# Attention with memory and a two-layer network on one core: unscaled exponentials and a division behind the product with V in the first two chunks

## The chip, the cores and the metric

The kernel runs on one core of a Trainium2 chip. The metric is the time of one execution on the device, in microseconds: 1301.19 us, the median of three runs (1300.96 to 1301.51). The profile shown is one further execution of the same kernel, taken with the hardware profiler.

The engines are named as the profile names them: PE is TensorE's matmul and PEld its load of a stationary operand, DVE is VectorE, ACT is ScalarE, POOL is GpSimd. Each of them works through its own list of instructions in order.

## What is computed

For 8 batches and 8 heads, with 576 positions of width 64, causal attention is mixed with a read of a memory matrix; the result, 4608 rows of 512, then goes through two weight matrices (512 x 2048 and 2048 x 512). Cut to what matters:

```
scores = q @ k.T / sqrt(D), causal;  a = exp(scores - max);  a /= a.sum(-1) + 1e-9
local = a @ v
q_p = phi(q)                      # phi(x) = max(x, 0) + min(exp(x), 1)
mem_out = (q_p @ M_prev) / (q_p @ z_prev + 1e-6)
g = 1 / (1 + exp(-beta))          # one number for each head
x = g * mem_out + (1 - g) * local
h = x @ w_in;  out = max(0.01 * h, h) @ w_out
```

q, k, v and the memory come as 32-bit floats, the weights as 64-bit floats.

## The kernel before, in words

A batch is done in two chunks of queries: chunk 0 of a batch has 320 queries against 320 keys (tiles of 64, 128 and 128 queries with 64, 192 and 320 keys), chunk 1 has 256 queries against 576 keys (two tiles of 128 with 448 and 576 keys). There are 16 chunks of 8 heads. The network of a chunk (class `Moe`, 16 steps of `first` and `second`) runs on TensorE while the next chunk's attention is done, and it splits every operand into a high and a low part, since its matmuls take a rounded 32-bit type: the low part is what rounding left over.

While the first two chunks run, the 32 weight tiles are converted from 64-bit floats: on each, `load_weight` spends two operations of ScalarE, three or four of VectorE (lines 290 to 301) and one or two of GpSimd. The attention of these two chunks (`full`, set by `PLAIN = 2`) runs in plain 32-bit floats on TensorE and needs no low parts of its operands.

One head of attention (`attention`): the score matmul (line 472), then `top` on VectorE (line 480) adds the mask and takes the row's extreme, `exp` on ScalarE (line 496) makes the exponentials and their sum, and then for each tile of queries three VectorE operations follow: `inv` (line 501) adds 1e-9 to the sum and multiplies it by 1/(1-g), `inv2` (line 506) takes the reciprocal, and `scale` (line 509) multiplies the whole row of exponentials by it. On GpSimd, `mem` (line 512) multiplies phi(q) by `rn`, the reciprocal of its product with z and of 1/g (lines 428 to 434), into 64 columns in front of the exponentials in the same tile `pp`. `turn` (line 526) transposes `pp` on TensorE in blocks of 128, ScalarE copies the blocks to `pt` (line 541), and `pv_full` (line 565) multiplies `pt` with M_prev and V, which lie one behind the other in `raw`. The result `o` is copied to its high part `xh` on ScalarE (line 568), and VectorE subtracts to get the low part `xl` (line 571), both as the network's input.

The order of the work isn't written by hand. `Plan` lists all steps with what they read and write, a duration each and a priority; a list schedule over the engines then sets the order on each engine, and that order is fixed when the program is built. Attention goes ahead of the weights in the first chunk, and the network's matmuls come last in priority. Tiles with a tag share a ring of buffers, so that a step waits until an earlier user of its buffer is done. TensorE's results lie in banks: `h` (one), `s` (one), `t` (a ring of two) and `acc0` to `acc3`.

## Time and profile before

| | |
|---|---|
| median of three runs | 1301.19 us |
| the profiled execution's span | 1298.5 us |
| PE, busy share of the span | 96% |
| DVE | 73% |
| ACT | 65% |
| POOL | 61% |

The runs' times include what lies around the span: the median is 2.7 us above the span shown, and the sums below are made against the span and then moved by these 2.7 us. The busy time of PE is that in which some matmul was in flight, so that PE can be busy and yet be fed too slowly. The page's 40 slices show the two stages of this kernel: in the first seven VectorE's digits are 7, 9, 9, 9, 8, 7 and 7 with PE between 7 and 8, and from there on PE stands at 9 to the end. When a row of a group gives a mean duration, successive operations of one engine overlap a little, so that the sum of durations is more than the time that they take.

### The profile page before, as it was taken

What the parts mean: (1) busy time and instruction counts of PE and PEld (TensorE: products, weight loads), DVE (VectorE), ACT (ScalarE), POOL (GpSimd) and SP (SyncE); (2) the same over time, 40 slices, a digit from 0 to 9 for tenths busy, and PEclk for the clock granted to TensorE, in tenths of its full rate; (3) what the DMA queues carried; (4) which work ended last, traced back from release to release, by engine and by line L of the source; (5) the groups of instructions that cost most, each with busy time, mean ns of one, the idle gap of its engine ahead of it and who ended that gap; (6) DMA issues with size and microseconds to landing.
All of it is one profiled execution on the core that took longest, in us unless ns stands there. A gap on an engine that the chain in (4) does not pass through costs nothing.

```text
span 1298.5 us, 26483 instructions
## 1 busy us (share of the span) xinstructions
PE 1243.6 (96%) x8896; PEld 1159.7 (89%) x8896; DVE 951.5 (73%) x3131; ACT 837.7 (65%) x2395; POOL 796.8 (61%) x1152
## 2 busy tenths in 40 slices
PE   7778889999999999999999999999999999999998
PEld 4566779999899999999999999999999999999998
DVE  7999877877788866778578785787767776777311
ACT  7656667766777766767576765667666675776322
POOL 4687757666666665756566665666657575666222
PEclk9899999999999999999999999999999999999999
DMA  6444422212222222222122221222221221212000
GB/s 240 156 145 152 152 74 70 98 68 74 91 82 93 66 70 77 80 88 70 38 96 84 79 70 51 87 69 90 70 74 69 87 79 41 98 65 81 1 21 17
DMA packets 32535, 107.61 MB, mean 83 GB/s; under 512 B 3728, under 2 KB 11920, under 8 KB 32400
## 3 DMA queue, kind: packets, MB, share of 16 engines
q1 hardware_dynamic: 32400, 105.92, 24.1%
q8 instruction: 71, 1.16, 0.4%
q14 instruction: 64, 0.52, 0.1%
HBM read 96.47 MB, written 9.44 MB: 82 GB/s over the span
## 4 chain that ended last, share of the span: by engine, by line
PE 69%; DVE 16%; POOL 6%; issue 5%; ACT 3%; DMA 0%; POOLq 0%; SPq 0%; ACTq 0%; DVEq 0%
PE h L620 24%; PE acc L620 24%; PE t L526 7%; PE o L584 6%; PE s L476 5%; DVE pp L509 3%; DVE pp L480 2%; PE s L472 2%; POOL gl L660 2%; DVE g L651 1%; ACT pp L496 1%; POOL qk L381 1%; DVE tawi L298 1%; DVE pt L544 1%; DVE tawo L298 1%
## 5 line engine op out<-in xcount | busy, mean ns | idle before, releaser
L620 PE MATMUL h<-xh,wih 128*128 128x256 f32 (+1 forms) x1024 | 321.4, 314 | 7.8 <-DVE g L651 6.0
L660 POOL TENSOR_TENSOR gl<-g,gh 128x320 fp32r<-128x320 f32 (+1 forms) x256 | 214.0, 836 | 184.3 <-ACT gh L655 158.1
L620 PE MATMUL acc<-gh,woh 128*128 128x256 f32 (+1 forms) x1024 | 321.1, 314 | 0.3
L620 PE MATMUL h<-xl,wih 128*128 128x256 f32 (+1 forms) x1024 | 302.6, 296 | 0.9 <-DVE xl L571 0.9
L620 PE MATMUL acc<-gl,woh 128*128 128x256 f32 (+1 forms) x1024 | 302.3, 295 | 0.9 <-POOL gl L660 0.8
L620 PE MATMUL h<-xh,wil 128*128 128x256 f32 (+1 forms) x1024 | 302.2, 295 | 0.0
L620 PE MATMUL acc<-gh,wol 128*128 128x256 f32 (+1 forms) x1024 | 301.5, 294 | 0.0
L496 ACT ACTIVATE pp<-pp,st 128x448 f32<-128x448 f32 (+3 forms) x320 | 180.4, 564 | 67.6 <-DVE st L480 61.9
L651 DVE TENSOR_TENSOR g<-h,g 128x320 f32<-128x320 f32 (+1 forms) x256 | 115.9, 453 | 135.2 <-ACT g L646 133.6
L646 ACT ACTIVATE g<-h 128x320 f32<-128x320 f32 (+1 forms) x256 | 104.7, 409 | 163.6 <-PE h L620 142.3
L620 PEld LDWEIGHTS h<-xh,wih 128*128 128x128 f32 x1024 | 193.4, 189 | 18.1 <-DVE g L651 10.9
L620 PEld LDWEIGHTS acc<-gh,woh 128*128 128x128 f32 x1024 | 193.0, 188 | 7.2 <-ACT os L693 1.5
L541 ACT CAST pt<-t 128x256 fp32r<-128x256 f32 (+4 forms) x392 | 141.1, 380 | 87.4 <-PE t L526 83.0
L620 PEld LDWEIGHTS acc<-gl,woh 128*128 128x128 f32 x1024 | 193.2, 189 | 3.8 <-POOL gl L660 1.8
L620 PEld LDWEIGHTS h<-xl,wih 128*128 128x128 f32 x1024 | 193.9, 189 | 2.5 <-DVE xl L571 1.5
L526 PE MATMUL t<-ident,pp 128*128 128x128 f32 (+1 forms) x960 | 168.1, 277 | 26.5 <-DVE pp L509 11.6
L620 PEld LDWEIGHTS h<-xh,wil 128*128 128x128 f32 x1024 | 193.2, 189 | 0.0
L620 PEld LDWEIGHTS acc<-gh,wol 128*128 128x128 f32 x1024 | 192.6, 188 | 0.0
L509 DVE TENSOR_SCALAR pp<-pp,st 128x448 f32<-128x448 f32 (+3 forms) x320 | 187.7, 587 | 5.5
L544 DVE TENSOR_TENSOR pt<-t,pt 128x256 fp32r<-128x256 f32 (+4 forms) x392 | 160.0, 426 | 31.2 <-ACT pt L541 28.7
L480 DVE CUSTOM_DVE_ANT_0 pp<-s,mask 128x448 f32<-128x448 f32 (+3 forms) x320 | 136.6, 428 | 47.7 <-PE t L526 23.0
L512 POOL TENSOR_TENSOR pp<-ph,st 128x64 f32<-128x64 f32 (+1 forms) x320 | 102.1, 324 | 107.7 <-DVE st L434 50.3
(63 smaller groups left out, 2252.9 us busy)
## 6 DMA issues: line engine op xcount, KB each, us to landing
raw<-raw SPq DMA_DIRECT2D x64, 672.0 KB, 4.0
raw<-raw SPq DMA_DIRECT2D x64, 544.0 KB, 3.6
wrwi<-w_in_bits SPq DMA_DIRECT2D x16, 512.0 KB, 3.5
wrwo<-w_out_bits SPq DMA_DIRECT2D x16, 512.0 KB, 3.3
out_t<-os SPq DMA_DIRECT2D x32, 160.0 KB, 1.8
out_t<-os SPq DMA_DIRECT2D x32, 128.0 KB, 1.7
braw<-beta_b SPq DMA_DIRECT2D x1, 4.0 KB, 1.6
```

The source lines that it names most:

```text
L480: nc.vector.tensor_tensor_reduce(out=pp()[:rw, D + k0 : D + k0 + kn], in0=s()[:rw, :kn], in1=mask[:rw, mo : mo + kn], scale=-0.0625 if ful ...
L496: nc.scalar.activation(out=pp()[:rw, D : D + n], in_=pp()[:rw, D : D + n], func=AF.Exp, scale=-1.0, bias=stat(kl_), accum_out=stat(2))
L509: nc.vector.tensor_scalar(out=pp()[:rw, D : D + n], in0=pp()[:rw, D : D + n], scalar1=stat(2), scalar2=None, op0=ALU.mult)
L512: nc.gpsimd.tensor_tensor(out=pp()[:rw, :D], in0=ph3()[:rw, ii, :], in1=rn()[:rw, ii : ii + 1].to_broadcast([rw, D]), op=ALU.mult)
L526: nc.tensor.transpose(t()[:, (j - j0) * rw : (j - j0 + 1) * rw], pp()[:rw, j * P : (j + 1) * P], ident[:rw, :rw])
L541: nc.scalar.copy(part(0), tv())
L544: nc.vector.tensor_tensor(out=part(1), in0=tv(), in1=f32r_bits(part(0)), op=ALU.subtract)
L584: nc.tensor.matmul(o()[:, c0[j] : nq], vt()[:, j, :], pt()[:, t, cols(j, c0[j]) : cols(j, nq)], start=n == 0, stop=n == len(mm) - 1)
L620: nc.tensor.matmul(dst(), l(), r(), start=start and k + j == 0, stop=stop and k + j == len(ops) - 1)
L646: op("ACT", act(n, True), q, lambda: nc.scalar.activation(out=g()[:, :n], in_=hp()[:, :n], func=AF.Copy, scale=0.01), r=[hp[0]], w=[g[0]])
L651: lambda: nc.vector.tensor_tensor(out=g()[:, :n], in0=hp()[:, :n], in1=g()[:, :n], op=ALU.max),
L660: lambda: nc.gpsimd.tensor_tensor(out=gl()[:, :n], in0=g()[:, :n], in1=f32r_bits(gh()[:, :n]), op=ALU.subtract),
```

## The change

In the first two chunks (`full`):

- `inv`, `inv2` and `scale` are gone. The exponentials stay unscaled in `pp`. When the last tile of a head has its sums, three small VectorE operations (`sum_1`, `sum_2`, `sum_3`) add 1e-9 to the sums of all tiles, multiply `rn` by them and take their reciprocals.
- `mem` now waits for `sum_2`, because the memory's part must be multiplied by the sum that is divided away later. The transposes of all tiles of a head (`turns`) are listed behind it.
- `v_gate` puts the gate on V: ScalarE multiplies the V part of `raw` by 1-g in place, in two operations, with a table `part` that is made once.
- `spread` transposes each tile's column of reciprocals, repeated over 128 columns, so that a bank `by` holds them along its columns on all rows: three transposes for a head in chunk 0, two in chunk 1. The bank is `h` in chunk 0 and one of the ring `t` in chunk 1.
- The product `o` is copied to a tile `x1` by ScalarE (`x_raw`), multiplied by `by` on VectorE (`x_div`), and then split: the high part on ScalarE as before, the low part on GpSimd (`x_lo`), no longer on VectorE.
- The first tile of chunk 0 is worked on with 128 rows instead of 64.

The diff's core, with comments left out:

```diff
+    part = cst.tile([P, 2, H], F32, name="part")
+    for k in range(2):
+        nc.vector.reciprocal(part[:, k, :], gate[:, 1, :])
+    nc.vector.memset(part[:D, 0, :], 1.0)
...
-        if not full:
+        if full:
+            def v_gate():
+                for j, (c, n) in enumerate(((0, 1), (1, nj - 1))):
+                    v = raw()[:, o_v + c * D : o_v + (c + n) * D]
+                    nc.scalar.activation(out=v, in_=v, func=AF.Copy, scale=part[:, j, h : h + 1])
+            op("ACT", 2 * act(nj * D // 2) + 190, prio, v_gate, r=[raw[0]], w=[raw["v"]])
+        else:
...
+            rows = P if full else rw
...
-            op("POOL", 300, prio, mem, r=[ph[0], st["n"]], w=[pp["f"]])
-            op("DVE", 129, prio, inv, w=[st["l", ii]])
-            op("DVE", 75, prio, inv2, w=[st["l", ii]])
-            op("DVE", dve2(n) + 40, prio, scale, r=[st["l", ii]], w=[pp["s", 0], pp["s", 1]])
+            if not full:
+                op("POOL", 300, prio, mem, r=[ph[0], st["n"]], w=[pp["f"]])
+                op("DVE", 129, prio, inv, w=[st["l", ii]])
+                op("DVE", 75, prio, inv2, w=[st["l", ii]])
+                op("DVE", dve2(n) + 40, prio, scale, r=[st["l", ii]], w=[pp["s", 0], pp["s", 1]])
+            later.append((ii, i, rw, rows, n, pp))
+            if not full:
+                turns(*later.pop())
+        if full:
+            sums = lambda: st()[:, 12 : 12 + ni]
+            def sum_1():
+                nc.vector.tensor_scalar(
+                    out=sums().unsqueeze(2), in0=st()[:, : 4 * ni].rearrange("p (i c) -> p i c", c=4)[:, :, 2:3], scalar1=1e-9, scalar2=None, op0=ALU.add
+                )
+            def sum_2():
+                nc.vector.tensor_tensor(out=rn(), in0=rn(), in1=sums(), op=ALU.mult)
+            def sum_3():
+                nc.vector.reciprocal(sums(), sums())
+            op("DVE", 129, prio, sum_1, r=[st["l", ii] for ii in range(ni)], w=[st["d"]])
+            op("DVE", 129, prio, sum_2, r=[st["d"]], w=[st["n"]])
+            op("DVE", 75, prio, sum_3, r=[st["n"]], w=[st["d"]])
...
+                op("POOL", 300, prio, mem, r=[ph[0], st["n"]], w=[pp["f"]])
+            for x in later:
+                turns(*x)
+        if full:
+            by = bank("t", 2, "by" + u) if hf else bank("h", 1, "by" + u)
...
+            x1 = tile_([P, 320], F32, "os", 1, "x1" + u)
+            def spread():
+                for ii, i in enumerate(tl):
+                    r = sums()[:, ii : ii + 1].to_broadcast([P, P])
+                    nc.tensor.transpose(by()[:, COL[i] : COL[i] + P], r, ident)
+            def x_raw():
+                nc.scalar.copy(x1()[a, :nq], o()[a, :nq])
+            def x_div():
+                nc.vector.tensor_tensor(out=x1()[a, :nq], in0=by()[a, :nq], in1=x1()[a, :nq], op=ALU.mult)
             def x_hi():
-                nc.scalar.copy(xh()[a, p, :], o()[a, :nq])
+                nc.scalar.copy(xh()[a, p, :], x1()[a, :nq])
             def x_lo():
-                nc.vector.tensor_tensor(out=xl()[a, p, :], in0=o()[a, :nq], in1=f32r_bits(xh()[a, p, :]), op=ALU.subtract)
+                nc.gpsimd.tensor_tensor(out=xl()[a, p, :], in0=x1()[a, :nq], in1=f32r_bits(xh()[a, p, :]), op=ALU.subtract)
```

How the instructions stand now, at three places (names: `pp_0_4_1` is chunk 0, head 4, tile 1; `raw`, `st`, `t`, `o`, `by` carry chunk and head likewise; a lone last number counts buffers, and lines are those of each kernel's own file).

VectorE, head 4 of the first chunk, from the first sum of its exponentials on. Before:

```order
L501 TENSOR_SCALAR st_0_4_377<-st_0_4_377,gate 64x1
L428 TENSOR_REDUCE st_0_5_404<-pz_0_5_372 128x3
L506 RECIPROCAL st_0_4_377<-st_0_4_377 64x1
L298 SCALAR_TENSOR_TENSOR tawo_282<-wrwo_214,tawo_282 128x512
L509 TENSOR_SCALAR pp_0_4_0_385<-pp_0_4_0_385,st_0_4_377 64x64
L501 TENSOR_SCALAR st_0_4_377<-st_0_4_377,gate 128x1 x2
L431 TENSOR_SCALAR st_0_5_404<-st_0_5_404,gate 128x3
L506 RECIPROCAL st_0_4_377<-st_0_4_377 128x1
L571 TENSOR_TENSOR xl_0_0_244<-o_0_3_393,xh_0_0_229 64x320
L509 TENSOR_SCALAR pp_0_4_1_390<-pp_0_4_1_390,st_0_4_377 128x192
L506 RECIPROCAL st_0_4_377<-st_0_4_377 128x1
L434 RECIPROCAL st_0_5_404<-st_0_5_404 128x3
```

and now:

```order
L580 TENSOR_SCALAR st_0_4_394<-st_0_4_394 128x3
L432 TENSOR_REDUCE st_0_5_443<-pz_0_5_392 128x3
L633 TENSOR_TENSOR x_0_3_438<-by_0_3_400,x_0_3_438 64x320
L585 TENSOR_TENSOR st_0_4_394<-st_0_4_394 128x3
L435 TENSOR_SCALAR st_0_5_443<-st_0_5_443,gate 128x3
L528 ISA pp_0_5_0_452,st_0_5_443<-s_0_5_0_0_429,mask 128x64
L528 ISA st_0_5_443 128x1
L588 RECIPROCAL st_0_4_394<-st_0_4_394 128x3
L438 RECIPROCAL st_0_5_443<-st_0_5_443 128x3
```

In place of three operations for each tile (501, 506, 509) there are three for the head (580, 585, 588), and the product of an earlier head with its spread reciprocals (633) stands where the subtraction (571) stood. Up to the last such row of the first chunk, eight weight tiles are ahead in VectorE's list now, and six were before.

GpSimd, around the first head of the second chunk. Before:

```order
L309 TENSOR_TENSOR wil_819<-tawi_726,wih_807 128x512
L660 TENSOR_TENSOR gl_0_2_839<-g_0_2_801,gh_0_2_822 128x320
L512 TENSOR_TENSOR pp_1_0_3_731<-ph_1_0_578,st_1_0_713 128x64
L512 TENSOR_TENSOR pp_1_0_4_768<-ph_1_0_578,st_1_0_713 128x64
L425 TENSOR_TENSOR pz_1_1_721<-ph_1_1_591,raw_1_1_145 128x128
L290 TENSOR_SCALAR tawi_864<-tawi_864 128x512
```

and now:

```order
L313 TENSOR_TENSOR wol_857<-tawo_751,woh_842 128x512
L596 TENSOR_TENSOR pp_1_0_3_747<-ph_1_0_645,st_1_0_739 128x64
L596 TENSOR_TENSOR pp_1_0_4_759<-ph_1_0_645,st_1_0_739 128x64
L313 TENSOR_TENSOR wil_891<-tawi_767,wih_868 128x512
L731 TENSOR_TENSOR gl_0_2_920<-g_0_2_862,gh_0_2_884 128x320
L313 TENSOR_TENSOR wol_931<-tawo_787,woh_915 128x512
```

The two products of phi(q) (512, now 596) stood behind nothing but their own phi; now they need the head's sums, and the weights' subtractions (313) and the network's (731) are queued behind them.

TensorE, heads 3 and 4 of the second chunk. Before:

```order
L526 MATMUL t_1_3_4_0_1375<-ident,pp_1_3_4_1296 128x128 x3
L526 MATMUL t_1_3_4_3_1382<-ident,pp_1_3_4_1296 128x128 x2
...
L620 MATMUL acc_0_1_740<-gh_0_8_1325,wol_1257 128x320
L472 MATMUL s_1_4_4_1_1401<-raw_1_4_966 128x256
L565 MATMUL o_1_3_1403<-pt_1_3_1333,raw_1_3_1135 64x256 x4
L565 MATMUL o_1_3_1403<-pt_1_3_1333,raw_1_3_1135 64x128
L526 MATMUL t_1_4_3_0_1423<-ident,pp_1_4_3_1352 128x128 x4
```

and now:

```order
L627 MATMUL by_1_3_1396<-ident,st_1_3_1224 128x128 x2
...
L619 MATMUL o_1_3_1409<-pt_1_3_1370,raw_1_3_1107 64x256 x4
L619 MATMUL o_1_3_1409<-pt_1_3_1370,raw_1_3_1107 64x128
L691 MATMUL h_0_8_1387<-xh_0_0_285,wih_1204 128x320
...
L691 MATMUL acc_0_2_819<-gh_0_7_1354,wol_1155 128x320
L473 MATMUL t_1_4_3_0_1455<-ident,pp_1_4_3_1323 128x128 x4
L473 MATMUL t_1_4_4_0_1464<-ident,pp_1_4_4_1348 128x128 x3
L691 MATMUL acc_0_3_826<-gh_0_7_1354,woh_1117 128x320
```

Before, head 4's first transposes (`t_1_4_3`) need the bank of head 3's middle block; now they need the bank of `by_1_3`, which comes free when head 3 has been divided (`x_div`). In both programs the same matmuls and transposes stand ahead of the second chunk's network (its first matmul, `h_1_0`), with the 40 spreading transposes added.

## Rows read from the trace of the kernel before

**Rows 1.** The table of stretches of the execution, core 0: the stretch from the span's start, its length, then for each engine the busy time and in brackets its instructions, the granted TensorE clock, the DMA share and GB/s.
```profile
0.00:10.00 10.00, 4.48 (x12) 2.87 (x12) 3.29 (x19) 4.76 (x15) 3.41 (x13) 1.00 0.79 296
10.00:50.00 40.00, 33.80 (x144) 18.51 (x143) 38.70 (x161) 29.78 (x105) 23.16 (x35) 0.96 0.51 182
50.00:160.00 110.00, 90.05 (x496) 73.19 (x496) 105.54 (x223) 65.55 (x148) 82.27 (x72) 0.95 0.44 150
160.00:178.00 18.00, 13.86 (x73) 10.36 (x72) 15.42 (x42) 9.20 (x22) 8.88 (x12) 0.91 0.20 72
178.00:300.00 122.00, 120.60 (x908) 115.27 (x908) 96.04 (x335) 86.90 (x258) 83.09 (x128) 1.00 0.25 84
300.00:1200.00 900.00, 887.63 (x6565) 847.89 (x6564) 672.27 (x2306) 610.48 (x1773) 571.12 (x862) 1.00 0.23 76
```

**Rows 2.** The waits in the first 180 us: who waited for whom; in total, how often, the longest.
```profile
POOL wol L309 <- ACT woh L306: 12.8, 6, 4.5
...
ACT wih L306 <- DVE tawi L301: 11.1, 10, 1.9
...
PE t L526 <- DVE pp L509: 8.7, 7, 1.8
```

**Rows 3.** The timeline around 175 us, VectorE's last row on the weights (start, length, what) and then TensorE's first matmul of the second chunk's mixture (its tile is 256 columns wide).
```profile
174.39 0.69 DVE L301 SCALAR_TENSOR_TENSOR tawo<-wrwo,tawo 128x512 int32<-128x512 int32 x1
...
177.76 0.39 PE L620 MATMUL h<-xh,wih 128*128 128x256 f32 x1 [1.11 <-DVE g L651]
```

**Rows 4.** VectorE's groups by line and shape in the first 180 us: those that the change takes away (count | busy us in sum, mean ns of one | idle before). The group with 64 rows holds one instruction of the third chunk beside the eight of the first, and 501 and 506 have 8 more instructions with 64 rows, not shown, of about the same length.
```profile
L509 DVE TENSOR_SCALAR pp<-pp,st 128x576 f32<-128x576 f32 x8 | 8.5, 1059 | 0.0
...
L501 DVE TENSOR_SCALAR st<-st,gate 128x1 f32<-128x1 f32 x32 | 6.5, 207 | 0.2 <-ACT pp L496 0.2
L509 DVE TENSOR_SCALAR pp<-pp,st 128x448 f32<-128x448 f32 x8 | 6.5, 812 | 0.0
...
L506 DVE RECIPROCAL st<-st 128x1 f32<-128x1 f32 x32 | 4.9, 153 | 0.1
...
L509 DVE TENSOR_SCALAR pp<-pp,st 64x64 f32<-64x64 f32 x9 | 4.0, 450 | 0.0
L571 DVE TENSOR_TENSOR xl<-o,xh 64x320 fp32r<-64x320 f32 x8 | 3.9, 487 | 0.6 <-ACT xh L568 0.4
L509 DVE TENSOR_SCALAR pp<-pp,st 128x192 f32<-128x192 f32 x8 | 3.8, 481 | 0.1
...
L509 DVE TENSOR_SCALAR pp<-pp,st 128x320 f32<-128x320 f32 x8 | 3.6, 447 | 0.0
...
L571 DVE TENSOR_TENSOR xl<-o,xh 64x256 fp32r<-64x256 f32 x8 | 3.3, 418 | 0.1
```

**Rows 5.** The timeline (start, length, what) of VectorE in four places and, as the row that begins at 143.26, of GpSimd: multiplications of line 509 at every width while nothing holds them, and one that begins while GpSimd is in a long operation.
```profile
44.57 0.24 DVE L509 TENSOR_SCALAR pp<-pp,st 64x64 f32<-64x64 f32 x1
44.73 0.15 DVE L506 RECIPROCAL st<-st 128x1 f32<-128x1 f32 x1
44.80 0.20 DVE L501 TENSOR_SCALAR st<-st,gate 128x1 f32<-128x1 f32 x1
44.92 0.68 DVE L298 SCALAR_TENSOR_TENSOR tawo<-wrwo,tawo 128x512 int32<-128x512 int32 x1
45.52 0.31 DVE L509 TENSOR_SCALAR pp<-pp,st 128x192 f32<-128x192 f32 x1
...
46.42 0.38 DVE L509 TENSOR_SCALAR pp<-pp,st 128x320 f32<-128x320 f32 x1
...
88.72 0.51 DVE L509 TENSOR_SCALAR pp<-pp,st 128x576 f32<-128x576 f32 x1
...
96.03 0.44 DVE L509 TENSOR_SCALAR pp<-pp,st 128x448 f32<-128x448 f32 x1
...
143.26 1.48 POOL L309 TENSOR_TENSOR wol<-tawo,woh 128x512 fp32r<-128x512 f32 x1 [0.58 <-ACT woh L306]
...
143.51 1.55 DVE L509 TENSOR_SCALAR pp<-pp,st 128x576 f32<-128x576 f32 x1
```

**Rows 6.** VectorE's groups again, same stretch and columns: the small operation on two and on three columns that stands nearest to the ones added.
```profile
L431 DVE TENSOR_SCALAR st<-st,gate 128x2 f32<-128x2 f32 x8 | 5.2, 649 | 0.1
...
L431 DVE TENSOR_SCALAR st<-st,gate 128x3 f32<-128x3 f32 x10 | 2.2, 222 | 0.0
```

**Rows 7.** GpSimd's groups, same stretch and columns: the subtraction whose shape is nearest to the one that moves there.
```profile
L660 POOL TENSOR_TENSOR gl<-g,gh 128x320 fp32r<-128x320 f32 x16 | 16.3, 1017 | 10.5 <-ACT gh L655 10.5
```

**Rows 8.** ScalarE's groups, same stretch and columns: copies of 64, 256 and 320 columns, and a weight tile's two operations.
```profile
L287 ACT ACTIVATE tawi<-wrwi 128x512 f32<-128x512 f32 x16 | 10.8, 673 | 0.0
...
L306 ACT CAST wih<-tawi 128x512 fp32r<-128x512 f32 x16 | 9.9, 618 | 11.3 <-DVE tawi L301 11.1
L541 ACT COPY pt<-t 128x256 f32<-128x256 f32 x24 | 8.6, 368 | 0.6 <-PE t L526 0.6
...
L568 ACT CAST xh<-o 64x320 fp32r<-64x320 f32 x8 | 3.4, 419 | 2.0 <-PE o L565 1.8
...
L541 ACT COPY pt<-t 128x64 f32<-128x64 f32 x8 | 1.7, 210 | 1.0 <-PE t L526 0.9
```

**Rows 9.** TensorE's timeline near the end of the second chunk: five transposes in a row, the product with V behind them (five matmuls, counted as ten records).
```profile
167.91 0.74 PE L526 MATMUL t<-ident,pp 128*128 128x128 f32 x5 [1.73 <-DVE pp L509]
169.08 3.65 PE L565 MATMUL o<-pt,raw 128*64 128x256 f32 x10 [0.44 <-ACT pt L541]
```

More of the change, by code (lines that the diff above doesn't have):

```diff
@@ L521, in attention, with turns, turn @@
+        later = []
+        def turns(ii, i, rw, rows, n, pp):
             for j0, js in BLOCKS[i]:
                 t = bank("t", 2, f"t{u}_{i}_{j0}")
-                def turn(t=t, js=js, j0=j0, rw=rw, pp=pp):
+                def turn(t=t, js=js, j0=j0, rw=rows, pp=pp):
                     for j in js:
@@ new lines, in attention, with mem @@
+        if full:
+            sums = lambda: st()[:, 12 : 12 + ni]
+            def sum_1():
+                nc.vector.tensor_scalar(
+                    out=sums().unsqueeze(2), in0=st()[:, : 4 * ni].rearrange("p (i c) -> p i c", c=4)[:, :, 2:3], scalar1=1e-9, scalar2=None, op0=ALU.add
+                )
+            def sum_2():
[5 more added lines that the diff above has]
+            op("DVE", 75, prio, sum_3, r=[st["n"]], w=[st["d"]])
+            for ii, i, rw, rows, n, pp in later:
+                def mem(ii=ii, pp=pp):
+                    nc.gpsimd.tensor_tensor(
+                        out=pp()[:, :D], in0=ph3()[:, ii, :], in1=rn()[:, ii : ii + 1].to_broadcast([P, D]), op=ALU.mult
+                    )
+                op("POOL", 300, prio, mem, r=[ph[0], st["n"]], w=[pp["f"]])
+            for x in later:
+                turns(*x)
```

111 lines of the change are left out of this document (56 added, 55 removed).

## Prediction

> **What bounds the kernel now.** I read the table of stretches first [rows 1]. Up to 178 us TensorE is not full: it idles 5.5 us of the first 10, 6.2 of the next 40, 20.0 of the 110 after that and 4.1 of the 18 up to 178, 35.8 us together. From there on it is busy for 120.6 us of 122 and 887.6 of 900. So the kernel is a start of 178 us that something else sets, and a rest of 1120.7 us (1298.5 less 177.8) that TensorE sets. In the same table VectorE is busy for 38.7 us of 40 and 105.5 of 110 while ScalarE has 29.8 and 65.6 and GpSimd 23.2 and 82.3: between 10 and 160 us VectorE is the full one. The waits agree [rows 2]: GpSimd waits for ScalarE's rounding of a weight, that rounding waits for VectorE's conversion of it, and TensorE's transposes wait for the scaling that VectorE does. VectorE's last conversion is at 174.39, and the second chunk's network begins at 177.76 [rows 3]. The listing of the order has the same matmuls ahead of that point in both programs, but for 40 spreading transposes. Whatever the change is worth must therefore show as an earlier or later start of that matmul, with the rest of 1120.7 us behind it unchanged.
>
> **What VectorE loses.** Successive rows overlap: a reciprocal of 0.15 begins at 44.73 and the next instruction at 44.80 [rows 5], so I take 0.08 off every instruction. The 40 scalings (line 509) are 8.5 + 6.5 + 3.8 + 3.6 us and 8 of 0.45, 26.0 in sum [rows 4], less 3.2 is 22.8. The 40 of line 501 at 0.207 are 8.3, less 3.2 is 5.1. The 40 reciprocals of line 506 at 0.153 are 6.1, less 3.2 is 2.9. The 16 subtractions (line 571) are 7.2, less 1.3 is 5.9. Together 36.7 us.
>
> **What VectorE gets.** `x_div` has the shape of line 571, with one operand in a bank and one tile, so I put it at the same 5.9 us. `sum_1` and `sum_2` are not in the trace. In chunk 0 they work on three columns, where line 431 takes 0.222 [rows 6]; with a reciprocal of 0.153 [rows 4] and three overlaps off that is 0.36 for a head, 2.9 us for eight. In chunk 1 they work on two, where line 431 takes 0.649 and single-column line 501 takes 0.207: 0.33 to 1.21 for a head, 2.6 to 9.7 us. I take the middle, 6.2, since `sum_2` is of another kind than either row. Added 15.0 us (11.4 to 18.5), net **21.7 us less** on VectorE (18.2 to 25.3). The table `part` is made near 3 us, before the first operands land, and costs nothing; if it were late, it would be three instructions of the size of line 501, 0.6 us.
>
> **What of it comes back.** First, the scalings wait as well as work. Free, they take 0.51, 0.44, 0.38, 0.31 and 0.24 at the five widths, 15.0 us for eight heads of each; the rows sum to 26.0, so 11.0 us are waiting. One that begins at 143.51 takes 1.55 while GpSimd is in an operation from 143.26 to 144.74 [rows 5]. Where the scaling is gone, VectorE's next instruction may meet the same GpSimd operation, so between 0 and 11.0 us come back; I take half, 5.5. Second, the 16 subtractions that move to GpSimd cost there 1.02 us at 320 columns [rows 7] and in proportion 0.81 at 256, 14.6 us. GpSimd has room for that (16.8 us idle in 40, 27.7 in 110 [rows 1]), but each can hold VectorE up: from 0 to half its length, 7.3 us. I take 2.5, nearer to none, because GpSimd has finished much of each before VectorE comes to an instruction that waits.
>
> What the Trainium skill says here ("SBUF — State Buffer", section "SBUF: two separate sides") is that VectorE and GpSimd share a pair of ports as an exclusive lock, held for a whole instruction, and that VectorE needs it in its two-port modes and also with two operands in SBUF. The row at 143.51 agrees. The rule also puts `sum_2` (two operands in SBUF) on the lock and keeps `x_div` (one in a bank) off it; by it alone the sums would stand at their upper end and the time 3.5 us higher.
>
> Third, the first chunk. Its share of the net is 11.0 us (24 scalings with 9.1 after overlaps, 24 of lines 501 and 506 with 4.8, less 2.9). ScalarE gets two operations on V and the copy `x_raw` for each head: 0.21 + 0.37 + 0.42 by copies of 64, 256 and 320 columns [rows 8], 1.0 us, 8 us in chunk 0 and as much in chunk 1. The listing also has two more weight tiles ahead of the last head of chunk 0, 0.67 + 0.62 each on ScalarE, 2.6 us. Against 10.2 us of idle ScalarE between 10 and 50 us that is 10.6: ScalarE is then full, and the chunk can't end much sooner than now. What VectorE saves there is used by the two tiles only, some 4 us (three operations of 0.60 for a tile, after overlap, and a fourth for every second one); between 0 and 7 us of the 11 are lost. I take 3. In chunk 1 ScalarE has 44 us idle of 110, and its 8 us lie beside VectorE.
>
> **What costs nothing.** The 40 spreading transposes at 0.15 (five in 0.74 [rows 9]) are 6 us on TensorE and lie in its 35.8 us of idle time; without that cover they'd cost 6. The first tile's 128 rows change no column count. `mem` now waits for `sum_2`; behind it GpSimd has weights and the network's subtractions queued, whose readers are TensorE's matmuls with the same cover. The bank `h` is taken by `by` through chunk 0, so nine early matmuls of the network move behind it, 9 x 0.15 = 1.3 us of the same idle time. `x1` is one buffer: `x_raw` waits for the `x_lo` of the head before, and the eight heads of chunk 1 are spread over some 120 us.
>
> **Sum.** 21.7 less 5.5, 2.5 and 3 is 10.7 us off the start. The profiled execution's span becomes 1287.8, and the median, 2.7 above the span, becomes **1290.5 us**. With every cost at its lower end it is 1301.2 - 25.3 = 1276, with every one at its upper end 1301.2 - 18.2 + 11.0 + 7.3 + 7 = 1308.
>
> **Rivals.**
>
> *The whole saving arrives.* VectorE has been the full engine for 150 us, and the others have idle time; if neither GpSimd's operations nor ScalarE take anything back, the time is 1301.2 - 21.7 = 1279.5. Against it: ScalarE's sum for chunk 0. Chance 0.18.
>
> *GpSimd's waits take it all back.* All 11.0 us of waiting move to other instructions, the moved subtractions add their 7.3 and the sums stand at 1.21 a head (3.5 more): 21.7 - 21.8 leaves nothing, 1301 us. For it: line 431 takes three times as long on two columns as on three [rows 6]. Against it: line 571 reads a bank and stands at 0.487 and 0.418 on the average [rows 4], no longer than its width asks. This is where the rule of the Trainium skill above would lead. Chance 0.10.
>
> *The transposes stand still, and it is slower.* In chunk 1 `by` and `o` take the ring `t` between one head's transposes and the next's, so TensorE stops in front of a head until the division of the last one is done: product with V (3.65 us in one case [rows 9]), copy, `x_div` behind whatever VectorE has queued. TensorE's busy time up to 178 us is 142.2 [rows 1]; with 6 us of transposes and the 5.5 us until the first operands, 24 us are left, so it decides from 3 us of standing for each of 8 heads. At 4 us each the start grows by 8, to 1309. For it: transposes already wait 8.7 us for the scaling in seven places [rows 2]. Against it: the network's matmuls stand between the heads in most places. Chance 0.06.
>
> **How the numbers follow.** The forecast has 0.66; its own range is 1283 to 1298. The range of 8 in 10 takes in the first rival's time and leaves out the other two: 1279 to 1299. A difference under 0.2% (2.6 us) can't be told from none in this kernel. Faster: the forecast but for 0.02 of its upper tail, the first rival and 0.01 of the second, 0.83. Same: 0.02 and 0.08, 0.10. Slower: 0.06 and the last 0.01, 0.07.
>
> **What would show it.** Right: the first 256-column matmul of the network starts near 167 us instead of 177.8, VectorE's busy time up to there falls by 12 to 20 us, the stretch behind it keeps its 1121 us, and the first chunk's attention ends about where it did. Wrong in a step: conversions of weights (lines 293 to 301 before) that take longer on average by over 0.1 us each would show the waits come back; ScalarE with idle time in the first 50 us would refute the third loss; gaps of several us in TensorE in front of the transposes of chunk 1, ended by `x_div`, would be the last rival. The forecast is wrong as a whole if the first network matmul of the second chunk moves by less than 3 or more than 21 us, or if the rest isn't 1121 us.

## The result, and the profile after

The changed kernel takes 1309.88 us (median of five runs, 1306.68 to 1312.3) against 1301.19: a ratio of 1.0056 [1.0044, 1.0068], 7.3 us slower by that ratio (the two medians are 8.7 us apart). The profiled execution has 1310.51 us and a span of 1308.7. Its table of stretches, with the columns of [rows 1]:

```profile
0.00:10.00 10.00, 4.52 (x12) 3.14 (x12) 2.95 (x17) 5.92 (x20) 2.62 (x10) 1.00 0.79 289
10.00:50.00 40.00, 29.99 (x144) 18.21 (x143) 34.15 (x120) 35.13 (x123) 27.93 (x43) 0.96 0.55 191
50.00:160.00 110.00, 94.11 (x494) 73.56 (x495) 94.94 (x193) 69.23 (x165) 85.56 (x79) 0.91 0.44 144
160.00:178.00 18.00, 15.50 (x90) 12.56 (x90) 16.68 (x42) 11.09 (x29) 13.38 (x14) 1.00 0.31 91
178.00:300.00 122.00, 119.81 (x894) 113.38 (x895) 97.89 (x339) 88.25 (x258) 82.36 (x128) 1.00 0.25 84
300.00:1200.00 900.00, 884.40 (x6528) 843.44 (x6527) 672.63 (x2283) 605.12 (x1758) 561.57 (x853) 1.00 0.23 75
```

VectorE is busy for 148.7 us of the first 178, where it was 163.0 [rows 1]: 14.2 less. Its idle time there rose by the same 14.2, from 15.1 to 29.3. Counted to the start of the second chunk's network in each kernel it is 150.2 us against 162.7, 12.5 less. The work went, and waits came. VectorE's last conversion and the second chunk's network (start, length, what), which answer to [rows 3], stand no earlier:

```profile
174.74 1.08 DVE L305 SCALAR_TENSOR_TENSOR tawo<-wrwo,tawo 128x512 int32<-128x512 int32 x1
...
181.73 0.39 PE L691 MATMUL h<-xh,wih 128*128 128x256 f32 x1
```

The network starts 4.0 us later, and from there to the end it takes 1308.7 - 181.7 = 1127.0 us, 6.3 more than the 1120.7 of before. So in these two profiles, whose spans are 10.2 us apart, two things went wrong, one on each side of that matmul.

The waits of the first 180 us (in total, how often, the longest) answer to [rows 2]:

```profile
ACT woh L310 <- DVE tawo L305: 14.4, 9, 3.3
...
DVE tawi L297 <- POOL tawi L294: 8.8, 3, 4.6
...
POOL wol L313 <- ACT woh L310: 7.8, 6, 2.3
...
PEld t L473 <- POOL pp L596: 6.4, 10, 1.7
```

VectorE now waits 8.8 us for GpSimd's `least` (1.1 us before), and TensorE's loads for the transposes (PEld) wait 6.4 us for GpSimd's `mem`. What VectorE got (count | busy us, mean ns | idle before), as [rows 4, 6] have it for what it had, and GpSimd's moved subtractions, as [rows 7]:

```profile
L585 DVE TENSOR_TENSOR st<-st 128x2 f32<-128x2 f32 x8 | 5.1, 635 | 0.1
...
L633 DVE TENSOR_TENSOR x<-by,x 64x320 f32<-64x320 f32 x8 | 3.9, 487 | 0.6 <-ACT x L630 0.2
...
L633 DVE TENSOR_TENSOR x<-by,x 64x256 f32<-64x256 f32 x8 | 3.3, 417 | 1.3 <-ACT x L630 1.2
L580 DVE TENSOR_SCALAR st<-st 128x3 f32<-128x3 f32 x8 | 3.1, 392 | 3.1 <-ACT pp L544 3.1
L580 DVE TENSOR_SCALAR st<-st 128x2 f32<-128x2 f32 x8 | 2.8, 350 | 0.0
...
L585 DVE TENSOR_TENSOR st<-st 128x3 f32<-128x3 f32 x8 | 1.2, 154 | 0.1
```
```profile
L639 POOL TENSOR_TENSOR xl<-x,xh 64x320 fp32r<-64x320 f32 x8 | 7.3, 912 | 3.5 <-ACT xh L636 3.3
...
L639 POOL TENSOR_TENSOR xl<-x,xh 64x256 fp32r<-64x256 f32 x8 | 6.7, 834 | 1.9 <-ACT xh L636 1.7
```

A useful mark inside the start is the network's first step: VectorE's first `g<-h,g`. It stands at 55.48 us before and at 66.10 after; the sixteenth at 177.22 and 181.19. Cut there, the two tables read (before, then after; columns as above):

```profile
0.00:55.48 55.48, 39.68 (x158) 22.07 (x158) 47.37 (x186) 37.19 (x125) 30.41 (x51) 0.94 0.60 213
55.48:177.22 121.74, 102.27 (x561) 82.62 (x561) 114.81 (x253) 71.33 (x164) 87.23 (x80) 0.96 0.39 133
```
```profile
0.00:66.10 66.10, 44.66 (x187) 28.20 (x188) 50.65 (x156) 50.02 (x164) 44.65 (x64) 0.87 0.55 195
66.10:181.19 115.09, 102.66 (x571) 82.20 (x571) 99.04 (x217) 74.38 (x177) 86.92 (x84) 0.97 0.41 132
```

The first step comes 10.6 us later; the stretch behind it is 6.7 us shorter. In that stretch VectorE does 15.8 us less, but TensorE's 102 us stay, and it has 12 us of idle time left in place of 19.

Where the 10.6 us arise can be read from TensorE's products with V of the last two heads of the first chunk, before:

```profile
45.43 1.59 PE L565 MATMUL o<-pt,raw 128*64 128x320 f32 x6
...
48.69 1.40 PE L565 MATMUL o<-pt,raw 128*64 128x320 f32 x6
```

and after, with what stands between the two:

```profile
46.03 1.40 PE L619 MATMUL o<-pt,raw 128*64 128x320 f32 x6
...
48.05 0.43 DVE L580 TENSOR_SCALAR st<-st 128x3 f32<-128x3 f32 x1
...
48.95 3.32 POOL L596 TENSOR_TENSOR pp<-ph,st 128x64 f32<-128x64 f32 x3 [0.50 <-DVE st L585]
...
52.33 0.90 PE L473 MATMUL t<-ident,pp 128*128 128x128 f32 x3 [1.22 <-POOL pp L596]
...
53.48 2.61 PE L619 MATMUL o<-pt,raw 128*64 128x320 f32 x6 [0.25 <-ACT pt L488]
```

The seventh product ends at 47.43 us against 47.02, so seven heads of the new kind lose 0.4 us together. The eighth ends 6.0 us later than before: its `mem` waits for the sums, then takes 3.32 us for three operations (0.92 for the head before it), and its transposes wait for `mem`. From the end of that product to the first step it takes 10.0 us instead of 5.4. How this last part goes shows in the timeline after (VectorE, GpSimd and ScalarE as named):

```profile
54.51 3.38 DVE L425 SCALAR_TENSOR_TENSOR ph<-ph,pz 128x128 f32<-128x128 f32 x1
...
55.27 1.25 POOL L313 TENSOR_TENSOR wil<-tawi,wih 128x512 fp32r<-128x512 f32 x1
...
56.17 0.42 ACT L630 COPY x<-o 64x320 f32<-64x320 f32 x1 [0.91 <-PE o L619]
56.49 1.25 POOL L313 TENSOR_TENSOR wol<-tawo,woh 128x512 fp32r<-128x512 f32 x1
...
59.38 0.49 DVE L633 TENSOR_TENSOR x<-by,x 64x320 f32<-64x320 f32 x1
...
59.94 0.64 PE L691 MATMUL h<-xh,wih 128*128 128x320 f32 x1 [3.85 <-DVE x L633]
60.37 0.47 PE L691 MATMUL h<-xl,wih 128*128 128x320 f32 x1
...
61.45 0.88 POOL L639 TENSOR_TENSOR xl<-x,xh 64x320 fp32r<-64x320 f32 x1
```

The copy `x_raw` is done at 56.59, but the division stands behind `phi_add` of the next chunk, which GpSimd's operations hold for 3.38 us, and behind two conversions. TensorE stands 3.85 us, then runs the first step's matmuls 0.27 us apart at a granted clock of 0.50 (54 to 60 us), the lower of its two levels.

### The profile page after: what moved, and what is told of

Its sections match the earlier page's. It is cut to its first block, busy times and chain, and to the rows that moved or that the text cites. A ratio compares the mean times of both kernels' runs of the same rounds, so it can differ in the third digit from the quotient of the medians.

```text
span 1308.7 us, 26566 instructions
## 1 busy us (share of the span) xinstructions
PE 1251.7 (96%) x8936; PEld 1166.1 (89%) x8936; DVE 946.7 (72%) x3062; ACT 852.9 (65%) x2443; POOL 806.9 (62%) x1168
## 4 chain that ended last, share of the span: by engine, by line
PE 53%; DVE 6%; POOL 5%; issue 4%; ACT 2%; DMA 1%; POOLq 0%; ACTq 0%
PE acc L691 19%; PE h L691 19%; PE t L473 5%; PE o L655 5%; PE s L524 4%; DVE pp L557 2%; POOL gl L731 2%; POOL qk L385 1%; DMA out_t<-os 1%; DVE pp L528 1%; DVE g L722 1%; POOL qk L388 1%; PE s L520 1%; ACT pp L544 1%; DVE pt L491 1%
## 5 line engine op out<-in xcount | busy, mean ns | idle before, releaser
L544 ACT ACTIVATE pp<-pp,st 128x448 f32<-128x448 f32 (+4 forms) x320 | 180.5, 565 | 74.3 <-DVE st L528 66.5
L528 DVE CUSTOM_DVE_ANT_0 pp<-s,mask 128x448 f32<-128x448 f32 (+4 forms) x320 | 136.8, 429 | 47.0 <-PE t L473 23.6
L557 DVE TENSOR_SCALAR pp<-pp,st 64x64 f32<-64x64 f32 (+4 forms) x280 | 161.5, 577 | 5.3
L473 PEld LDWEIGHTS t<-ident,pp 128*128 128x128 f32 (+1 forms) x960 | 114.3, 141 | 43.2 <-issue 7.8
```

The costliest lines, as they stand in the source:

```text
L473: nc.tensor.transpose(t()[:, (j - j0) * rw : (j - j0 + 1) * rw], pp()[:rw, j * P : (j + 1) * P], ident[:rw, :rw])
L528: nc.vector.tensor_tensor_reduce(out=pp()[:rw, D + k0 : D + k0 + kn], in0=s()[:rw, :kn], in1=mask[:rw, mo : mo + kn], scale=-0.0625 if ful ...
L544: nc.scalar.activation(out=pp()[:rw, D : D + n], in_=pp()[:rw, D : D + n], func=AF.Exp, scale=-1.0, bias=stat(kl_), accum_out=stat(2))
L557: nc.vector.tensor_scalar(out=pp()[:rw, D : D + n], in0=pp()[:rw, D : D + n], scalar1=stat(2), scalar2=None, op0=ALU.mult)
```

## The experiments

The ratio is to the kernel before on the same chip, and 0.001 is 1.3 us. The last three columns are us, each of one profile.

| kernel | ratio [95%] | first step | second chunk's network | from there to the end |
|---|---|---|---|---|
| before | | 55.5 | 177.8 | 1120.7 |
| after | 1.0056 [1.0044, 1.0068] | 66.1 | 181.7 | 1127.0 |
| e1 second chunk only | 1.0027 [1.0018, 1.0036] | 56.8 | 180.1 | 1125.2 |
| e2 first chunk only | 1.0050 [1.0035, 1.0065] | 65.1 | 180.7 | 1126.6 |
| e3 no gate | 1.0069 [1.0055, 1.0083] | 65.7 | 183.6 | 1125.7 |
| e4 mem without sums | 1.0070 [1.0056, 1.0085] | 65.3 | 183.2 | 1127.0 |
| e5 before again | 1.0004 [0.9994, 1.0014] | 55.6 | 178.0 | 1122.0 |
| e6 before, no scaling, second | 0.9965 [0.9952, 0.9978] | 58.1 | 174.2 | 1122.6 |
| e7 before, no scaling, first | 0.9967 [0.9954, 0.9980] | 51.1 | 173.3 | 1122.3 |
| e8 sums spread in ring t | 1.0100 [1.0083, 1.0117] | 70.0 | 185.5 | 1129.3 |
| e9 after, old later order | 1.0045 [1.0031, 1.0060] | 65.7 | 182.8 | 1123.0 |
| e10 division ahead | 1.0071 [1.0058, 1.0084] | 65.3 | 183.6 | 1127.6 |
| e11 tile by tile | 1.0028 [1.0019, 1.0037] | 57.0 | 179.0 | 1126.0 |
| e12 x_lo on VectorE | 1.0032 [1.0021, 1.0044] | 63.1 | 177.0 | 1126.2 |
| e13 e1 with x_lo on VectorE | 1.0006 [0.9998, 1.0015] | 60.0 | 180.5 | 1122.9 |
| e14 before, no scaling at all | 0.9931 [0.9917, 0.9945] | 51.3 | 168.4 | 1122.3 |
| e15 scaling of second on ScalarE | 0.9956 [0.9944, 0.9969] | 54.5 | 171.1 | 1122.0 |
| e16 and the wide ones of first | 0.9976 [0.9967, 0.9985] | 56.5 | 175.3 | 1121.7 |
| e17 before, new later order | 1.0048 [1.0034, 1.0061] | 57.6 | 182.1 | 1126.5 |
| e18 e12 with old later order | 1.0015 [1.0006, 1.0024] | 63.2 | 177.4 | 1123.4 |

**One half of the change at a time.** In e1 and e2 everything that the change adds or takes is made to hang on `new`:

```diff
         full = plain(b, hf)
+        new = full and hf in (1,)     # e2: (0,)
...
-        if full:
+        if new:
             def v_gate():
```

> The change is made in the second chunk alone; the first chunk scales its exponentials as before. Theory A (the first chunk's attention, whose head is now a longer chain through ScalarE, VectorE and GpSimd, ends 10 us later and the start never gets that back): the second chunk's network starts 2 to 8 us before that of the kernel before (170 to 176 us against 177.8), and the time is 1294 to 1300. Theory B (GpSimd, which takes mem behind the sums and the moved subtractions in the second chunk, is the bound there): the network starts at 178 to 184 and the time is 1302 to 1310. Theory C (the later chunks' order, which the planner works out anew, is 6 us worse whatever happens in the start): the time from the network's start to the end is 1126 to 1128 here too, against 1120.7.

> The change is made in the first chunk alone. Theory A: the first chunk's network starts some 10 us later, as in the changed kernel (first step at 66 us against 55.5), the second chunk's network 4 to 10 us later than before, and the time is 1305 to 1312. Theory B: the loss of the first chunk is filled with weights, the second chunk's network starts within 2 us of 177.8, and the time is 1300 to 1303. Theory C: from the network's start to the end 1126 to 1128.

Both halves are slower by themselves. The 10 us of the first step come with the first chunk's half alone, as theory A has it, but only 2.9 us of them reach the second chunk's network (theory A had 4 to 10), and theory A's gain of e1 isn't there: e1 is where theory B put it. Both also take 1125 to 1127 us behind the network's start. Theory C, a new order there, can be the reason in e2 alone, since e1 has the order of before in that stretch.

**The suspected engine loads.** e3 leaves the products of V with the gate out, e4 the products `sum_2`; the order of all other instructions stays.

```diff
-                    nc.scalar.activation(out=v, in_=v, func=AF.Copy, scale=part[:, j, h : h + 1])
+                    pass                                                              # e3
...
-                nc.vector.tensor_tensor(out=rn(), in0=rn(), in1=sums(), op=ALU.mult)
+                pass                                                                  # e4
```

> The changed kernel in its own order, but V is not multiplied by the gate: 32 ScalarE instructions, 10.3 us, are gone. Theory A by way of a full ScalarE (35.1 us of 40 busy between 10 and 50 us): the first chunk ends 3 to 5 us earlier, the second chunk's network starts 3 to 5 us earlier than in the changed kernel, time 1304 to 1307. If ScalarE isn't what holds the first chunk: under 1.5 us, 1308 to 1311.

> The changed kernel in its own order, but the 16 products of the sums with the denominators of phi are left out, so that GpSimd's mem no longer waits for VectorE's sums, and VectorE has 16 instructions less (7 us). If VectorE's work still set the start, the second chunk's network would start 5 to 7 us earlier than in the changed kernel and the time would be 1303 to 1305. If the waits of GpSimd's queue for the sums are what makes VectorE idle (theory B), more than that, 8 to 12 us, time 1298 to 1302. If both lie beside something else (theory A through the chain of copy, division, rounding), 0 to 3 us, 1307 to 1310.

Neither gives anything back, though e3 frees ScalarE of 32 instructions and e4 VectorE of 16. So neither of these two pieces of work is what the start of the changed kernel waits for.

**What the removed work is worth.** e5 is the kernel before, unchanged. e6, e7 and e14 are the kernel before with scalings left out and nothing in their place.

```diff
             def scale(rw=rw, n=n, pp=pp, stat=stat):
+                if (b, hf) == (0, 1):          # e7: (0, 0); e14: if plain(b, hf)
+                    return
```

> The kernel before, unchanged, once more in a profile, because the stretch from the second chunk's network to the end took 1125 to 1127 us in all four variants and 1120.7 before, though the variant of the second chunk alone has the same instructions in the same order there on every engine. Theory D (that stretch scatters from execution to execution, and the 1120.7 was at its lower end): 1122 to 1126 here. Theory E (the changed kernels are slower there, by the place of their tiles in memory or by what the start leaves behind): 1120 to 1121.5. The network's start at 177.8 within 1 us by both.

> The kernel before in its own order, with the 16 scalings of the second chunk left out (some 12 us of VectorE) and nothing put in their place. Theory F (VectorE's work sets the start, as the prediction had it): the second chunk's network starts 8 to 12 us earlier, 166 to 170, time 1290 to 1294. Theory G (from the first network step, near 55 us, TensorE's own work and its waits in order set the pace, 102 us busy of 122, and VectorE only looks full): 0 to 4 us earlier, 174 to 178, time 1298 to 1302.

> The kernel before in its own order, with the 24 scalings of the first chunk left out (some 9 us of VectorE) and nothing put in their place. Theory F: the network's first step 7 to 9 us earlier than 55.5 us and the second chunk's network 7 to 9 us earlier too, time 1293 to 1295. Theory G with a first chunk that is a chain from head to head: the first step 2 to 6 us earlier, and the second chunk's network 2 to 6 us, time 1296 to 1300.

> The kernel before in its own order with all 40 scalings left out and nothing put in their place. If the start is a row of two stretches that each have their own chain, the two gains add: the first network step near 51, the second chunk's network at 169 to 171, time 1292 to 1294.5. If VectorE's work counted in full once both are gone (theory F): 155 to 160, time 1280 to 1284. If something else steps in: 172 to 174, time 1296 to 1298.

e5 takes 1122.0 us behind the network's start, 1.3 more than the same kernel's first profile, at the lower edge of theory D: two profiles of one kernel differ by that much. The halves are worth 4.6 us (e6) and 4.3 (e7), both together 9.0: they add, and theory F falls. (e6's 1296.6 us, by its ratio, lies below theory G's range too.) Cut at the first step as above, e14 reads:

```profile
0.00:51.26 51.26, 37.05 (x158) 21.34 (x158) 39.32 (x161) 36.76 (x125) 31.68 (x51) 0.98 0.66 230
51.26:167.86 116.60, 101.75 (x561) 84.47 (x561) 106.39 (x236) 70.07 (x163) 85.27 (x80) 0.95 0.42 139
```

The scalings had 26.0 us of busy time, 22.8 without overlaps [rows 4]; VectorE's busy time falls by 16.5 and the start by 9.4. The first stretch gives 4.2 us and the second 5.1, where TensorE's 102 us stay.

**The chain of a head in the first chunk.** e8 moves the spread sums to the ring `t`, e10 moves the last division ahead of the three instructions in front of it, and e11 leaves `sum_2` out and lists `mem` and the transposes of a tile beside its exponentials.

```diff
-            by = bank("t", 2, "by" + u) if hf else bank("h", 1, "by" + u)
+            by = bank("t", 2, "by" + u)                                               # e8
...
+        x = [o for o in done if o.fn.__name__ == "x_div"][7]
+        ahead = [o for o in done[: done.index(x)] if o.eng == "DVE"][-3:]
+        done = again(lambda o: x.start + 1 if o in ahead else o.start)                # e10
...
+            if full:
+                op("POOL", 300, prio, mem_, r=[ph[0], st["n"]], w=[pp["f"]])          # e11
...
-            if not full:
-                turns(*later.pop())
+            turns(*later.pop())
```

(`again` lists the steps anew by the key it is given, each behind those it needs.)

> The changed kernel with the spread sums of the first chunk in the ring t and not in bank h, so that the network's first matmuls can go ahead of the last heads again. If bank h is what delays the first network step (66.1 us against 55.5): the step at 60 to 63 us, the second chunk's network 2 to 4 us earlier than 181.7, time 1305 to 1308. If it is the head's longer chain and the ring gets fuller: the step at 66 to 69 us, time 1309 to 1313.

> The changed kernel with one instruction moved: the last division of the first chunk goes ahead of the three VectorE instructions that stood before it (phi_add of the second chunk, held 3.4 us, and two conversions of a weight). If that block is a loss that the start never gets back: the network's first step 2.5 to 3.5 us earlier than 66.1 us, the second chunk's network 2 to 3.5 us earlier than 181.7, time 1306 to 1308. If TensorE's stretch behind it only gets its idle time back: first step 2.5 to 3.5 us earlier, the second chunk's network under 1 us, time 1309 to 1310.5.

> The changed kernel without the product of the sums with the denominators of phi, so that mem and the transposes of a tile need its own exponentials only and are listed tile by tile, as before the change, and not behind the sums of the whole head. If it is the head that waits as a whole (theory A, the longer chain in the first chunk): the first network step falls from 66.1 to 57 to 61 us, the second chunk's network from 181.7 to 174 to 178, time 1301 to 1305. If the chain behind the product with V (copy, division, rounding, GpSimd's subtraction) is what costs: 63 to 66 us, 180 to 183, time 1308 to 1311.

e8 is worse than either reading had it (70.0 us and, by the ratio, 1314.2), so bank `h` alone isn't what delays the first step. In e10 the division and TensorE's first matmul come 3.3 us earlier, and the first step only 0.8; the timeline of e10 shows why:

```profile
56.12 0.49 DVE L651 TENSOR_TENSOR x<-by,x 64x320 f32<-64x320 f32 x1 [2.04 <-ACT x L648]
...
56.67 0.64 PE L709 MATMUL h<-xh,wih 128*128 128x320 f32 x1 [1.09 <-DVE x L651]
...
58.56 0.62 ACT L328 CAST woh<-tawo 128x512 fp32r<-128x512 f32 x1 [2.47 <-DVE tawo L323]
...
59.20 0.46 ACT L654 CAST xh<-x 64x320 fp32r<-64x320 f32 x1
...
60.60 0.86 POOL L657 TENSOR_TENSOR xl<-x,xh 64x320 fp32r<-64x320 f32 x1
```

The rounding `x_hi` now stands in ScalarE's queue behind a weight that waits 2.47 us for the conversions that were moved back. So moving one step of the chain ahead left the next one waiting in another engine's queue. e11 takes some 9 us off the first step, where e4, with the same omission and the order kept, got 0.8: in the first chunk it is the listing by whole heads that costs, as far as one new listing of everything can show it. Its last product with V ends at 45.4 us, 10.7 earlier than after, and the chain from there to the first step still takes 11.6. Of the 9 us only 2.7 reach the second chunk's network, at 179.0 later than the 174 to 178 expected. The time falls by 3.6 us against after and by 2.2 against e9, which has the same later order; the last two intervals overlap.

**The subtractions on GpSimd.** e12 puts `x_lo` back on VectorE, e13 does so in e1, e18 does so in e9.

```diff
-                nc.gpsimd.tensor_tensor(out=xl()[a, p, :], in0=x1()[a, :nq], in1=f32r_bits(xh()[a, p, :]), op=ALU.subtract)
+                nc.vector.tensor_tensor(out=xl()[a, p, :], in0=x1()[a, :nq], in1=f32r_bits(xh()[a, p, :]), op=ALU.subtract)
```

> The changed kernel with the 16 subtractions x_lo on VectorE, as they were, and not on GpSimd. If GpSimd's queue and the operands that both engines want are what holds the start up: the first network step 1 to 3 us earlier than 66.1, the second chunk's network 2 to 5 us earlier than 181.7, time 1304 to 1308, though VectorE does 7 us more. If VectorE's work counts (the prediction's premise): the network 3 to 6 us later, time 1312 to 1316. If neither, within 1.5 us of 1309.9.

> The change in the second chunk alone, with the 8 subtractions x_lo on VectorE and not on GpSimd. If the moved subtractions are what takes the saving back there: the second chunk's network starts 3 to 6 us earlier than the 180.1 of the second chunk alone, 174 to 177, the stretch behind it takes 1122 to 1123.5 (it has the old order), time 1297.5 to 1301.5. If it is the longer chain of the head (sums, mem, copy, division): within 2 us of 180.1, time 1304 to 1307.

Three pairs agree: 0.0024 (after and e12), 0.0021 (e1 and e13), 0.0030 (e9 and e18), 2.7 to 3.9 us (each ratio is good to some 0.0012), though VectorE does more. The planner lists the first two chunks anew each time, so this is the price of the move with the order that goes with it. VectorE's group of line 297 in the first 180 us, after and then in e12, shows the wait that goes:

```profile
L297 DVE TENSOR_SCALAR tawi<-tawi 128x512 int32<-128x512 int32 x16 | 9.5, 611 | 8.9 <-POOL tawi L294 8.8
```
```profile
L297 DVE TENSOR_SCALAR tawi<-tawi 128x512 int32<-128x512 int32 x16 | 10.4, 654 | 0.7 <-POOL tawi L294 0.6
```

e12 is where its first reading put it; e13's time lies between its two readings and can't be told from before. In its one profile e13 started its network no earlier than e1 (180.5), but that execution is 2.6 us above e13's median, and the last section has a part of what delayed it.

**The order of the later chunks.** e9 is the changed kernel with every instruction of the later chunks in the order of before; e17 is the reverse. The old (new) starts in the plan are written into the kernel.

```diff
+        was = {(tuple(x[:4]), x[4]): x[5] for x in json.loads(...)}
+        first = [o for o in done if o.key in was and o.key[0][3] == 2][0]
+        by = first.start - was[first.key]
+        done = again(lambda o: was[o.key] + by if o.key in was else o.start)
```

> The changed kernel with its own order in the first two chunks, but every instruction of the later chunks (third chunk's attention and second chunk's network onwards) is put in the order that it has in the kernel before, on every engine. Theory H (the later chunks' order, which the planner made anew, costs the stretch behind the start some 4 us): from the network's start to the end 1121 to 1123.5, as in the four kernels that have that order by themselves (1120.7, 1122.0, 1122.3, 1122.6), and the time 1304 to 1306.5. Theory I (something else than the order, such as the place of the tiles in memory; the variant of the second chunk alone has that order too and took 1125.2): 1125 to 1127, time 1308 to 1311. The network's start at 181 to 183.5 by both.

> The kernel before, its work and its first two chunks untouched, but every instruction of the later chunks in the order that the changed kernel has there. Theory H (the order costs it): the network of the second chunk at 177 to 179, from there to the end 1125.5 to 1127.5, time 1304.5 to 1307. Theory I (the order doesn't matter, the work of the start or the place of the tiles does): 1120.5 to 1123, time 1300.5 to 1303.

> The changed kernel with its subtractions x_lo on VectorE and the later chunks in the old order. If the two effects add: network at 176 to 178.5, from there 1121 to 1123.5, time 1300 to 1303.5, no different from before. If theory I holds: 1125 to 1127 behind the start, time 1304 to 1307.

The stretch behind the network's start in e9 and in e17:

```profile
182.82:1305.80 1122.98, 1102.56 (x8179) 1055.61 (x8177) 789.87 (x2693) 728.83 (x2107) 678.60 (x1022) 1.00 0.22 71
```
```profile
182.12:1308.60 1126.48, 1104.66 (x8177) 1057.22 (x8177) 795.10 (x2690) 728.11 (x2103) 675.87 (x1020) 1.00 0.21 71
```

With the same matmuls the old order takes 1123 and the new one 1126.5, which is theory H's side. Not all of e17's length is the order's: its first 6 us of that stretch ran at the lower clock, those of before at the higher (e17, then before):

```profile
182.12:188.00 5.88, 5.88 (x25) 5.82 (x25) 1.95 (x9) 2.52 (x8) 3.57 (x6) 0.52 0.32 98
```
```profile
177.76:183.60 5.84, 5.74 (x42) 5.37 (x42) 2.45 (x11) 3.69 (x13) 5.44 (x8) 1.00 0.31 91
```

TensorE has 25 matmuls there in place of 42, and at the 60th matmul e17 is 1.9 us behind. In time the order is worth 1.4 us (after and e9, whose intervals overlap), 2.2 (e12 and e18) and 6.2 (e17 against before; there the network also starts 4.3 us later than before, outside the 177 to 179 expected, so that this isn't the price of the stretch alone). e9's 1307.0 us, by its ratio, misses theory H's time, and e18 ends 2 us above before, not level with it. Ten profiles in the old order took 1120.7 to 1123.4, but e1 and e11, which have it too, 1125.2 and 1126.0. What those two lost is spread over many places; its cause is open.

**Another way to the same saving.** e15 keeps the kernel before, but ScalarE does the second chunk's scalings; in e16 also the eight of 320 keys.

```diff
             def scale(rw=rw, n=n, i=i, pp=pp, stat=stat):
+                if plain(b, hf) and hf == 1:          # e16: and (hf == 1 or i == 2)
+                    p = pp()[:rw, D : D + n]
+                    nc.scalar.activation(out=p, in_=p, func=AF.Copy, scale=stat(2))
+                    return
```

> The kernel before with the 16 scalings of the second chunk on ScalarE (some 10 us of its 44 idle ones between 50 and 160 us) and not on VectorE. If VectorE's work in the second chunk is worth what leaving it out showed: the network 2 to 4 us earlier than 177.8, time 1297.5 to 1300. If ScalarE's place in the chain of a head costs as much: within 1.5 us of 177.8, time 1300.5 to 1303.

> As e15, and the 8 widest scalings of the first chunk (320 keys) on ScalarE too, some 3.5 us of the 10 that it idles between 10 and 50 us. If the first chunk's chain is shortened by that: the first network step 1 to 3 us earlier than 55.5, the network of the second chunk 4 to 6 us earlier than 177.8, time 1295 to 1298. If ScalarE is then what the heads wait for: the first step at 55.5 or later, time as e15 or longer.

e15 beats both kernels: 1296.7 us, 5.7 us (0.9956) under before. Its stretch from 50 to 160 us has ScalarE 10 us busier than [rows 1] and VectorE 4 us less:

```profile
50.00:160.00 110.00, 91.88 (x516) 74.72 (x516) 101.35 (x224) 75.53 (x171) 83.10 (x78) 0.97 0.46 152
```

That is as much as e6 got by leaving the same scalings out (4.6 us). The planner lists the first two chunks anew in e15, and the granted clock of this stretch is 0.97 in place of 0.95, so how much the move itself is worth isn't shown. In e16 the first step isn't earlier, and it gives half of the gain back.

## Why the prediction was wrong

**The sizes on VectorE were right.** The prediction took 13.7 us off VectorE (21.7 less 5.5 and 2.5); its busy time up to the second chunk's network fell by 12.5. `x_div` stands at 0.487 and 0.417 as forecast, the moved subtractions at 14.0 us against 14.6. The sums are 14.7 us of rows, some 10.9 without 48 overlaps, against 9.1. The Trainium skill's rule of the shared ports ("SBUF — State Buffer", section "SBUF: two separate sides") agrees. `sum_2`, with two operands in SBUF, takes 0.14 to 0.16 us in eleven of sixteen cases and 0.75 to 1.25 in five, each of which begins inside a GpSimd operation and ends with it, as here:

```profile
118.91 1.29 POOL L313 TENSOR_TENSOR wol<-tawo,woh 128x512 fp32r<-128x512 f32 x1 [2.31 <-ACT woh L310]
119.21 1.01 DVE L585 TENSOR_TENSOR st<-st 128x2 f32<-128x2 f32 x1
```

Two more begin inside GpSimd's `least` and aren't held. `phi_add`, also with two, was held for 3.38 us, and `x_div`, with one operand in a bank, is never held.

**The step that failed first** is the premise of its first part, that whatever VectorE loses must show as an earlier start because VectorE is the full engine. e14 measures the exchange: of 22.8 us of scalings left out, 16.5 leave VectorE's busy time (6.3 come back, near the 5.5 that the prediction took), and the start is 9.4 us earlier. A share of busy time of 96% over 110 us didn't mean that VectorE set the end of the stretch. What sets it was argued and not measured: behind the first step TensorE is busy for 102 us of the 115 to 122 in a fixed order, and ahead of it each head is a chain through all engines.

**The second step that failed** is in "What costs nothing". `mem` and the transposes were costed for the work they hold up and the bank they take, not for being listed behind the sums of the whole head. It is the larger failure: at e14's rate, 9.4 us for 16.5, the 12.5 us off VectorE would still have been a gain of some 7 (an estimate). The last head's wait and the copy, division and subtraction behind its product put the first step 6.0 and 4.6 us later, where the prediction had the first chunk end about where it did. The third loss, a full ScalarE that costs 3, was the wrong cause: ScalarE idles 4.9 us of 40 there, and e3 gave nothing.

**The third** is "the rest of 1120.7 us unchanged". The planner lists all chunks in one go, so that a change in the first chunk alone (e2) already gives the later chunks another order; beside their partners the new orders took 4.0 us more (after and e9), 2.8 (e12 and e18) and 5.8 (e17 and before), some 2 of the last at the lower clock.

One path through the kernels divides the 7.3 us, in ratios to before (such steps sum to the whole by construction, so the sum itself proves nothing): no scalings, -9.0 us (e14); the division by sums in their place, +10.9 (e14 to e18); `x_lo` on GpSimd, +3.9 (e18 to e9); the later order, +1.4 (e9 to after). How the 10.9 divide among sums, spreading, copy and listing wasn't measured apart; e11 against e9 gives the listing, with `sum_2`, some 2 of them, at the edge of what the ratios tell.

**The rivals.** The first one, the whole saving at 1279.5, rests on the same premise and falls with it. The last one had the time (1309), by luck, but not the place: TensorE waits 0.6, 2.1 and 3.85 us for a division in the first chunk, and 0.2 once in the second. The second one's price for the moved subtractions was bounded at 7.3, taken at 2.5, and is 2.7 to 3.9.

## What to carry to other kernels

Before a full engine's work is counted as time, leave that work out with the order kept and nothing in its place: here 22.8 us of scalings, the largest of what the change takes away, were worth 9 us before a line of the new scheme was needed. Idle time on another engine doesn't make a move there free either: the scalings of the second chunk on ScalarE came with a gain (e15), eight more with a loss (e16), and the subtractions on GpSimd with a loss of 2.7 to 3.9 us. New steps behind the last product of a chain cross several queues, each with other work in it. Where a planner lists the whole program, a change at the start is also a new order for the rest, and it is to be costed or kept out.

## What wasn't expected of the chip

The kernel before and e17 have the same instructions in the same order in the first chunk, but e17's first step is 2.1 us later. The difference begins at TensorE's scores of the third head (before, then e17):

```profile
5.51 4.97 PE L472 MATMUL s<-raw 128*64 128x64 f32 x12 [5.51 <-DMA raw<-raw]
...
12.12 1.39 PE L472 MATMUL s<-raw 128*64 128x64 f32 x6
```
```profile
5.10 4.96 PE L1382 MATMUL s<-raw 128*64 128x64 f32 x12 [5.10 <-DMA raw<-raw]
...
11.84 2.48 PE L1382 MATMUL s<-raw 128*64 128x64 f32 x6
```

The twelve records of the first two heads take 4.97 us in both, 2.48 for six. The next six take 1.39 us before and still 2.48 in e17; e6 and e13 have the 2.48 too. The granted clock's column reads 1.00 from 6 to 18 us in all of them, but it also reads 1.00 where the trace has no record of the clock, and the first record, at the full level, begins at 11.71 us before, at 15.62 in e6, 17.44 in e13 and 17.15 in e17. In all twenty profiles a record of 320 columns takes 0.74 us until about that moment and 0.43 behind it. So TensorE's early matmuls run at the lower of its two levels, 1.2 of 2.4 GHz, and the rise came 6.2 us after the first matmul in one execution and 12.1 in another of the same work in the same order, with the engine busy all the while. A first step in one profile is good to some 2 us for that reason, and the comparisons above that rest on less go by the ratios.
